# A top-k attention with a feed-forward layer: the first pair of slots projects another unit, two early slots search by pairs, one slot copies x later

## The chip, the cores and the metric

The kernel runs on one core of a Trainium2 chip. The metric is the device time of one execution in microseconds (us). Before the change the median of three runs is 1456.52 us (1456.08 to 1456.63). The engines are named as in the profile: PE is TensorE (PEld its weight loads), DVE is VectorE, ACT is ScalarE, POOL is GpSimd, SP is SyncE, whose queue issues most DMAs.

## What is computed

The reference, cut to what matters:

```python
B, H, S, D = 8, 8, 576, 64
scores = (q @ k.transpose(0, 1, 3, 2)) / np.sqrt(D)
kth = np.partition(scores, -32, axis=-1)[..., -32:-31]
scores = np.where(scores >= kth, scores, -1e9)
attn = np.exp(scores - scores.max(-1, keepdims=True))
attn = attn / (attn.sum(-1, keepdims=True) + 1e-9)
x = (attn @ v).transpose(0, 2, 1, 3).reshape(B * S, H * D)     # 4608 x 512
h = x @ w_in                                                   # 512 x 2048
out = (h / (1 + np.exp(-1.702 * h))) @ w_out                   # 2048 x 512
```

Each row of scores keeps its 32 largest of 576. All matrices are float32.

## The kernel before

**Slots.** The attention is cut into 144 slots, 18 for each batch. A slot holds 128 query rows of two heads (or the 64 left-over rows of two pairs of heads). For slot n the engines do, in this order: TensorE makes the scores (`scores`, L295) into two `s_ps` tiles; ScalarE copies them to `sc` (`copy_scores`, L307); VectorE finds the 32 largest of each row; ScalarE masks (L423) and takes the exponentials with their sums (L431); VectorE inverts the sums (L439, L441); the probabilities are turned, multiplied with v on TensorE (`values`, L526, or `values_at`, L557), and ScalarE copies the result into x (L539, L571).

**Two ways to search.** `topk` works on the 576 scores of a row: eight times MAX8 (L317) and six times MATCH_REPLACE8 (L320) for the two halves of a slot. `topk_of_pairs` works on 288 pairs: `pair_up` puts the greater of each pair into `greater` on VectorE (L336) and starts the lesser on GpSimd (L339), `pair_rest` ends the lesser (L349); then the greater ones are searched as above on half the width (L366, L369), two more rounds go over the lesser ones, and two small reductions (L373, L378) give `top` and the bound `cut`. In the middle of its search it calls `pair_up` for the next slot. After a plain search `bounds` computes `cut` and `low` on GpSimd (L410, L411); after a search by pairs only `low` is left for GpSimd (`lows`, L399).

**Stages.** Slots 0 to 10 are issued one by one by `slot`, with the plain search; their probabilities are turned on TensorE by a scaled identity (`divide`, L448 on GpSimd; `turn`, L468, L471), and ScalarE copies the turned tiles (L476). In these slots the weights are also rounded: `round_piece` gives, for each of 32 pieces, ScalarE operations `size` (L151), `sign` (L153) and `low` (L154), a VectorE `shift` (L152) and two GpSimd operations `finish` (L144, L147). Pieces 0 to 15 are `w_in`; pieces 16 to 31 are the sixteen rows `f` of `w_out`. From slot 11 on `two_slots` issues pairs of slots, with the search by pairs; the probabilities are normalized on GpSimd (`normalize`, L454), split into halves by ScalarE (`split`, L490), and turned by two DMAs in SP's queue (L492, L498).

**Feed-forward.** When four pairs of heads of 128 rows are done, their x is a block (`ready`). A block is worked off in four units of four `f`. `hidden` makes a unit's hidden values `ph` on TensorE (L618); `tanh` on ScalarE takes their tanh (L640), and from slot 11 on also copies `ph` to `h` (L643); `gate` multiplies, on VectorE in slots up to 10 (L655) and on GpSimd afterwards (L652, L653); `project` takes the oldest gated unit from `to_project` and adds four products with `wout` into the block's `po` (L673). After a block's last unit `leave` scales it into `ob` (L681) and sends it out (L683). `may_project` lets a unit be issued only when the `finish` operations of its rows of `wout` are already issued.

**Buffers in PSUM.** `ps_t` has two buffers, shared by the turns, the transposes of q and k for later batches (`prepare_main`, L217, copied by ScalarE at L218; `prepare_ends`, L222), the products `o`, and such `ph` as `hidden` puts there. `ps_h` has one buffer, for `ph`; `ps_p` has one, for `po`. When a block is projected for the first time, `project` gives it `ps_p`, or `ps_h` if another block still has `ps_p`; as long as a block has `ps_h`, `hidden` uses `ps_t`, and for one more call afterwards (`pos["rest"]`).

**Order.** The order is written by hand: in `manual_schedule` each engine runs its instructions in the order in which the program issues them, and waits by semaphores for what they read or overwrite.

In `measure(m)` the bounds of slot m are followed by `pair_rest()` and `gate(aside)`; a pair ends with `tanh(aside)`, `measure(n + 1)`, `project_one()` and `leave_all()`. `opens` is true in the pair of slots 11 and 12, `aside` in all pairs that have slots.

Of the kernel before, what the change touches and what calls it, by code (L numbers as in the profile page):

```python
# [11 lines left out]
F32 = mybir.dt.float32  # L12
# [6 lines left out]
P = 128  # L19
# [11 lines left out]
def kernel(  # L31
# [36 lines left out]
    HALF = S // 2  # L68
# [15 lines left out]
    TURNS = 4  # L84
    SETTLED = 10
    PAIRED = SETTLED + 1
    assert D == 64 and 2 * TAIL == P and C == NP * P and C == PIECE and B % 2 == 0
    assert TOPK == 32 and NP == 4 and NF == 4 and NG == 4 and CC == 4

# [27 lines left out]
    raw = {}  # L117
# [191 lines left out]
    def topk(n):  # L309

        sc = st[n]["sc"]
        top = st[n]["top"] = small.tile([P, 2, TOPK], F32, name="top")
        left = [lefts.tile([P, S], F32, name="left") for _ in range(2)]
        of = lambda r, i: left[i][:] if r else sc[:, i, :]

        def largest(r, i):
            nc.vector.max(top[:, i, 8 * r : 8 * r + 8], of(r, i))  # L317

        def remove(r, i):
            nc.vector.match_replace(left[i][:], top[:, i, 8 * r : 8 * r + 8], of(r, i), LOWEST)  # L320

        ops = []
        for r in range(TOPK // 8):
            ops += [lambda r=r, i=i: largest(r, i) for i in range(2)]
            if r < TOPK // 8 - 1:
                ops += [lambda r=r, i=i: remove(r, i) for i in range(2)]
        return ops
# [3 lines left out]
    def pair_up(n):  # L331

        sc = st[n]["sc"]
        a, b = sc[:, :, 0:HALF], sc[:, :, HALF:S]
        greater[n] = lefts.tile([P, 2, HALF], F32, name="greater", tag="left")
        nc.vector.tensor_tensor(out=greater[n][:], in0=a, in1=b, op=ALU.max)  # L336
        lesser[n] = raws.tile([P, 2, HALF], F32, name="lesser", tag="raw")
        whole = lesser[n][:].bitcast(I32)
        nc.gpsimd.tensor_tensor(out=whole, in0=a.bitcast(I32), in1=greater[n][:].bitcast(I32), op=ALU.subtract)  # L339
        unpaired.append(n)  # L340
# [10 lines left out]
    def topk_of_pairs(n):  # L351

        top = st[n]["top"] = small.tile([P, 2, 2 * TOPK], F32, name="top2", tag="top")
        cut = st[n]["cut"] = small.tile([P, 2], F32, name="cut")
        first, few = greater.pop(n), lesser.pop(n)
        left = lefts.tile([P, 2, HALF], F32, name="left2", tag="left")

        def found(r, i, written=False):
            if r < TOPK // 8:
                at = (8 * r + TOPK) % (TOPK + TOPK // 2)  # L360
                return top[:, i, at : at + 8]
            end = 2 * TOPK - 8 * (r - TOPK // 8) - TOPK
            return top[:, i, end - 1 : end - 9 : -1] if written else top[:, i, end - 8 : end]

        def largest(src, r, i):
            nc.vector.max(found(r, i, True), src[:, i, :])  # L366

        def remove(to, src, r, i):
            nc.vector.match_replace(to[:, i, :], found(r, i), src[:, i, :], LOWEST)  # L369

        def merge():
            both = top[:, :, 0:TOPK].rearrange("p i (s k) -> p i k s", s=2)
            nc.vector.tensor_reduce(  # L373
                out=top[:, :, TOPK + TOPK // 2 :], in_=both, axis=mybir.AxisListType.X, op=ALU.max
            )

        def bound():
            nc.vector.tensor_reduce(  # L378
                out=cut[:], in_=top[:, :, TOPK + TOPK // 2 - 1 :], axis=mybir.AxisListType.X, op=ALU.min, negate=True
            )  # L380

        ops = []
        for r in range(TOPK // 8):
            ops += [lambda r=r, i=i: largest(left if r else first, r, i) for i in range(2)]
            if r < TOPK // 8 - 1:
                ops += [lambda r=r, i=i: remove(left, left if r else first, r, i) for i in range(2)]
        ops += [lambda: pair_up(n + 1) if n + 1 < N else None]
        for r in range(TOPK // 8, TOPK * 3 // 16):
            ops += [lambda r=r, i=i: largest(few, r, i) for i in range(2)]
            if r == TOPK // 8:  # L390
                ops += [lambda r=r, i=i: remove(few, few, r, i) for i in range(2)]
        return ops + [merge, bound]
# [9 lines left out]

    def bounds(n):

        if n >= PAIRED:
            return lows(n)
        top = st[n]["top"]
        cut = st[n]["cut"] = small.tile([P, 2], F32, name="cut")
        low = st[n]["low"] = small.tile([P, 2], F32, name="low")
        nc.gpsimd.tensor_scalar(cut[:], top[:, :, TOPK - 1], -1.0, None, op0=ALU.mult)  # L410
        nc.gpsimd.tensor_tensor(out=low[:], in0=top[:, :, TOPK - 1], in1=top[:, :, 0], op=ALU.subtract)  # L411

    def exponentials(n, between=lambda: None):

        mask(n)
        between()
        exps(n)
# [239 lines left out]
            )  # L657
        to_project.append((th, g, blocks))

    def project(put_off_leaving=False):  # L660

        gT, fs, blocks = to_project.pop(0)
        for x in blocks:
            if not x.done:
                home = "ps_h" if "ps_p" in in_use else "ps_p"
                in_use.append(home)
                x.home = home
                pool_of, tag = (ps_h, "ph") if home == "ps_h" else (ps_p, "po")
                x.po = pool_of.tile([P, C], F32, name="po", tag=tag)
        i = 0  # L670
        for f in fs:
            for x in blocks:
                nc.tensor.matmul(  # L673
                    x.po[:], lhsT=gT[:, i * P : (i + 1) * P], rhs=wout[:, f, :], start=(x.done == 0), stop=(x.done == FC - 1)
                )
                x.done += 1
                i += 1

        def leave(x):
            ob = thp.tile([P, C], F32, name="ob", tag="th")  # L680
            nc.scalar.mul(out=ob[:], in_=x.po[:], mul=0.5 / RAISE**2)  # L681
            for on, to in x.rows:
                nc.sync.dma_start(to, ob[on, :])  # L683

        for x in blocks:
            if x.done == FC:
                in_use.remove(x.home)
                leaving.append(lambda x=x: leave(x))
        if not put_off_leaving:
            leave_all()  # L690
# [49 lines left out]
    def finish_one():  # L740
        unfinished.pop(0)()
# [74 lines left out]
    def slot(n):  # L816
# [7 lines left out]
        if n == 0:  # L824
            for piece in some:
                piece["low"]()
                piece["sign"]()
        else:
            bounds(n - 1)
            exponentials(n - 1, bring_all if n % 4 == 1 else lambda: None)  # L830
            copy_scores(n + 1)
            bring_all()
            while signs:
                signs.pop(0)()
            if 1 < n <= TURNS:
                turn_main(n - 2)
                turn_ends(n - 2)
            for piece in some:
                piece["size"]()
            tanh(False)  # L840
        for i, op in enumerate(topk(n)):
            op()
            if i == 2:
                for _ in range(min(3 if n >= TURNS else 6, len(unfinished))):
                    finish_one()
            if i == 5:
                if n > 0:
                    divide(n - 1)
                while unfinished:
                    finish_one()  # L850
            if i == 10:
                gate(False)
        if n == SETTLED:
            pair_up(n + 1)
            pair_rest()
        for piece in some:
# [2 lines left out]
        if n < NP:  # L859
            for fn, args in preparing:  # L860
                fn(*args)
        if n >= TURNS:
            turn_main(n - 1)
            turn_ends(n - 1)
        if n > 0:
            for piece in some:
                piece["low"]()
        scores(n + 2)
        if n == SETTLED:
            copy_scores(n + 2)  # L870
# [32 lines left out]
    def two_slots(n):  # L903
# [27 lines left out]
        def measure(m):  # L931
            if live(m):
                lows(m)
            pair_rest()
            gate(aside)

        def project_one():
            if may_project(0):
                project(True)

        if opens:
            bounds(n - 1)
            gate(aside)
        if ahead:
            scores(n + 2)
# [26 lines left out]
        for piece in some:  # L972
            piece["shift"]()
            piece["low"]()
            piece["sign"]()
            unfinished.extend(piece["finish"])
        if live(n - 1):
            split(n - 1)
        begin(todo[0])
# [26 lines left out]
        find(n + 1)  # L1006
        if live(n):
            normalize(n)
            split(n)
        begin(todo[1])  # L1010
        if live(n):
            turn_by_dma(n)
        tanh(aside)
        measure(n + 1)
        project_one()
        leave_all()

    with tc.manual_schedule():
# [37 lines left out]
```

## Time and profile before

| | before |
|---|---|
| median of three runs | 1456.52 us |
| the profiled execution | 1456.39 us |
| its span, first to last instruction | 1454.6 us |
| PE busy | 1416.5 us (97%) |
| DVE busy | 1362.5 us (94%) |
| ACT busy | 1158.9 us (80%) |
| POOL busy | 977.6 us (67%) |
| mean granted TensorE clock | 0.986 |

Slot 0's search begins at 9.41 us, slot 10's ends at 132.99 us. In the 40 equal slices of the span (36.4 us each) the page gives, in tenths:

```profile
PE   7789799999999999999999999999999999999998
DVE  7999999999999999999999999999999999999910
PEclk8899899999999999999999999999999999999999
```

A page or a timeline row reads: start, length, engine, line of the kernel, operation, output and inputs with their sizes, count; in brackets the idle time of the engine just before, and whose end released it. The windows give for a stretch of time each engine's busy time, and the clock that TensorE was granted as a share of the full one. The chain is followed back from the last instruction, at each step to what released it or to the instruction before it on its engine.

### The profile page before, as it was taken

The page shows a single profiled execution, that of the slowest core. Times are in us where ns is not written, and L with a number is a line of the kernel's source. Part 1 is how long each engine was busy: PE and PEld are TensorE (multiplying, and loading weights), DVE is VectorE, ACT ScalarE, POOL GpSimd, SP SyncE. Part 2 cuts the span into 40 slices and gives each one's busy share as a digit, 9 for nine tenths or more (in the row PEclk, how much of TensorE's full clock was granted, in tenths as well). Part 3 has the DMA queues.
Part 4 walks back from the last instruction along what each step waited for, and adds up shares of the span by engine and source line. Part 5 has one row for each costly group of instructions (what it writes and reads, how often), then busy time and mean ns, then how long its engine had stood idle before and what let it go on. Part 6 is the DMA issues. An engine that isn't in the chain of part 4 may idle for free.

```text
span 1454.6 us, 29079 instructions
## 1 busy us (share of the span) xinstructions
PE 1416.5 (97%) x9524; PEld 996.4 (68%) x9524; DVE 1362.5 (94%) x4681; ACT 1158.9 (80%) x1862; POOL 977.6 (67%) x1177
## 2 busy tenths in 40 slices
PE   7789799999999999999999999999999999999998
PEld 5667466777666667777666667777666667777665
DVE  7999999999999999999999999999999999999910
ACT  6998787888888887888888888888878888777730
POOL 3788766766677777666777777766777767667610
PEclk8899899999999999999999999999999999999999
DMA  7442467777777867777677767767677776645430
GB/s 224 136 161 75 127 154 191 189 189 180 176 198 184 188 170 191 186 198 177 170 194 182 183 170 195 202 174 189 166 203 189 180 182 179 161 133 130 138 89 15
DMA packets 521272, 244.40 MB, mean 168 GB/s; under 512 B 457376, under 2 KB 495264, under 8 KB 521120
## 3 DMA queue, kind: packets, MB, share of 16 engines
q1 hardware_dynamic: 520688, 242.25, 64.4%
q8 instruction: 75, 1.23, 0.3%
q14 instruction: 77, 0.63, 0.2%
q10 hardware_dynamic: 432, 0.30, 0.1%
HBM read 45.09 MB, written 103.42 MB: 102 GB/s over the span
## 4 chain that ended last, share of the span: by engine, by line
PE 87%; DVE 10%; ACT 2%; POOL 0%; issue 0%; DMA 0%; DVEq 0%; POOLq 0%; ACTq 0%
PE ph L618 33%; PE po L673 32%; PE o L557 10%; PE s_ps L295 10%; DVE top L317 4%; DVE left L320 3%; DVE top L366 1%; DVE left L369 1%; ACT sc L490 0%; ACT sc L423 0%; ACT pr L431 0%; DVE wout L152 0%; PE none L169 0%; ACT sc L307 0%; DMA pt<-rows 0%
## 5 line engine op out<-in xcount | busy, mean ns | idle before, releaser
L618 PEld LDWEIGHTS ph<-xT,win 128*128 128x128 f32 x3520 | 484.2, 191 | 85.2 <-issue 54.6
L618 PE MATMUL ph<-xT,win 128*128 128x128 f32 (+1 forms) x3520 | 537.1, 309 | 0.5 <-ACT xT L574 0.5
L673 PE MATMUL po<-wout,th 128*128 128x512 f32 x1152 | 521.0, 595 | 5.6 <-POOL wout L147 5.6
L490 ACT COPY sc<-pr 128x2304 uint16<-128x2304 uint16 x134 | 283.1, 2113 | 170.3 <-POOL pr L454 170.3
L673 PEld LDWEIGHTS po<-wout,th 128*128 128x128 f32 x1152 | 213.6, 191 | 219.0 <-issue 205.8
L366 DVE MAX8 top<-left 128x8 f32<-128x288 f32 x798 | 323.2, 446 | 0.0
L339 POOL TENSOR_TENSOR lesser<-sc,greater 128x576 int32<-128x576 int32 x133 | 188.4, 1417 | 179.8 <-DVE greater L336 179.8
L454 POOL TENSOR_SCALAR pr<-pr,rden 128x576 f32<-128x576 f32 x268 | 196.6, 746 | 126.7 <-DVE top L373 77.7
L369 DVE MATCH_REPLACE8 left<-top,left 128x288 f32<-128x288 f32 x532 | 231.3, 442 | 0.0
L431 ACT ACTIVATE pr<-sc,low 128x576 f32<-128x576 f32 x288 | 220.8, 774 | 0.0
L366 DVE MAX8 top<-lesser 128x8 f32<-128x288 f32 x532 | 214.9, 445 | 0.0
L423 ACT ACTIVATE sc<-sc,cut 128x576 f32<-128x576 f32 x288 | 207.4, 774 | 6.2 <-POOL cut L410 6.2
L307 ACT ACTIVATE sc<-s_ps 128x576 f32<-128x576 f32 x288 | 170.9, 648 | 34.2 <-PE s_ps L295 32.6
L349 POOL TENSOR_TENSOR lesser<-lesser,sc 128x576 int32<-128x576 int32 x133 | 187.8, 1412 | 0.1
L295 PE MATMUL s_ps<-qk_t 64*128 64x288 f32 (+1 forms) x1280 | 183.7, 433 | 0.5 <-ACT qk_t L218 0.3
L653 POOL TENSOR_TENSOR th<-th,h 128x512 f32<-128x512 f32 x131 | 167.5, 1279 | 10.9
L295 PEld LDWEIGHTS s_ps<-qk_t 64*128 64x128 f32 (+1 forms) x1280 | 100.2, 179 | 79.2 <-issue 59.0
L557 PE MATMUL o<-pt,v_l 128*64 128x128 f32 (+1 forms) x2400 | 145.8, 265 | 2.1 <-DMA pt<-rows 1.9
L557 PEld LDWEIGHTS o<-pt,v_l 128*64 128x64 f32 x2400 | 121.4, 137 | 29.5 <-issue 17.7
L336 DVE TENSOR_TENSOR greater<-sc 128x576 f32<-128x576 f32 x133 | 131.9, 992 | 0.0
L652 POOL TENSOR_SCALAR th<-th 128x512 f32<-128x512 f32 x131 | 81.5, 622 | 59.7 <-ACT th L640 59.7
L640 ACT ACTIVATE th<-ph 128x512 f32<-128x512 f32 x144 | 85.5, 593 | 38.0 <-PE ph L618 33.9
(78 smaller groups left out, 1365.5 us busy)
## 6 DMA issues: line engine op xcount, KB each, us to landing
rows<-sc SPq DMA_DIRECT2D x134, 576.0 KB, 3.2
qk_rows<-halves SPq DMA_DIRECT2D x48, 256.0 KB, 2.8
qk_l<-in_q_dram SPq DMA_DIRECT2D x64, 128.0 KB, 3.4
raw<-in_moe_w_in_dram SPq DMA_DIRECT2D x16, 512.0 KB, 4.7
v_l<-in_v_dram SPq DMA_DIRECT2D x32, 256.0 KB, 3.7
raw<-in_moe_w_out_dram SPq DMA_DIRECT2D x16, 512.0 KB, 3.5
out_dram<-ob SPq DMA_DIRECT2D x32, 256.0 KB, 2.9
qk_l<-in_k_dram SPq DMA_DIRECT2D x62, 128.0 KB, 3.4
```

The costliest lines, as they stand in the source:

```text
L295: nc.tensor.matmul(ps[i][rows, c, 0:HALF], lhsT=qT[b, hps[p]][on, cols], rhs=kT[b, hps[p]][on, FIRST[i] + c * HALF : FIRST[i] + (c + 1) * ...
L339: nc.gpsimd.tensor_tensor(out=whole, in0=a.bitcast(I32), in1=greater[n][:].bitcast(I32), op=ALU.subtract)
L349: nc.gpsimd.tensor_tensor(out=whole, in0=whole, in1=b.bitcast(I32), op=ALU.add)
L366: nc.vector.max(found(r, i, True), src[:, i, :])
L369: nc.vector.match_replace(to[:, i, :], found(r, i), src[:, i, :], LOWEST)
L423: nc.scalar.activation(sc[:, i, :], sc[:, i, :], AF.Prelu, bias=cut[:, i : i + 1], alpha=HUGE)
L431: nc.scalar.activation(pr[:, i * S : (i + 1) * S], sc[:, i, :], AF.Exp, bias=low[:, i : i + 1], accum_out=den[:, i : i + 1],)
L454: nc.gpsimd.tensor_scalar(pr[:, i, :], pr[:, i, :], st[n]["rden"][:, i : i + 1], 1.0, op0=ALU.mult, op1=ALU.mult)
L490: nc.scalar.copy(out=halves, in_=pr[:].bitcast(U16).rearrange("p (k h) -> p h k", h=2))
L557: nc.tensor.matmul(o[j * D : (j + 1) * D, cols], lhsT=main[:, j, c, :] if c < NF else tail[:, j, :], rhs=pt[:, MAIN[j] + c if c < NF else ...
L618: nc.tensor.matmul(ph[:, i * many * P : (i + 1) * many * P], lhsT=win[:, c, f * P : (f + 1) * P], rhs=xs[:, first : first + step * (many - ...
L673: nc.tensor.matmul(x.po[:], lhsT=gT[:, i * P : (i + 1) * P], rhs=wout[:, f, :], start=(x.done == 0), stop=(x.done == FC - 1))
```

## The change

- `by_pairs` says which slots are searched by pairs: now also slots 1 and 2 (`EARLY`). Their `lesser` lives in the pool of `sc` rather than that of the raw weights. The slot before such a slot calls `bounds` for itself, then `pair_up` and `pair_rest`, at the end of its own search; that holds for slot 10 too, whose `bounds` came after slot 11's `pair_up` before.
- Slot 5 (`TURNS + 1`) copies x (`bring_all`) behind the exponentials and not between the mask and them, and gates its unit after operation 13 of its search, not 10. Slot 4 issues two of its three `low` operations ahead of the turns of slot 3.
- In the first pair, slot 11's `measure` finishes the pieces that are left (one whole piece of `wout`) and gates nothing; the last piece's `finish` follows at once instead of during the search of slot 12. `measure` of slot 14 gates twice.
- At the end of the first pair `project(True, 1)` takes the second unit in `to_project`, the first of the next block, where `project_one` took the oldest, the last of the first block. That one is projected by the next pair.
- In the pair of slots 13 and 14 the `tanh` of the second half stands ahead of slot 13's `split`.

The core of the diff:

```diff
+    EARLY = (1, 2)
+    by_pairs = lambda n: n in EARLY or PAIRED <= n < N
...
-        lesser[n] = raws.tile([P, 2, HALF], F32, name="lesser", tag="raw")
+        home, tag = (scp, "sc") if n in EARLY else (raws, "raw")
+        lesser[n] = home.tile([P, 2, HALF], F32, name="lesser", tag=tag)
...
-        ops += [lambda: pair_up(n + 1) if n + 1 < N else None]
+        ops += [lambda: pair_up(n + 1) if PAIRED < n + 1 < N else None]
...
-    def project(put_off_leaving=False):
+    def project(put_off_leaving=False, which=0):
-        gT, fs, blocks = to_project.pop(0)
+        gT, fs, blocks = to_project.pop(which)
...
-            bounds(n - 1)
-            exponentials(n - 1, bring_all if n % 4 == 1 else lambda: None)
+            if not by_pairs(n):
+                bounds(n - 1)
+            exponentials(n - 1, bring_all if n % 4 == 1 and n > TURNS + 1 else lambda: None)
+            if n == TURNS + 1:
+                bring_all()
...
-        for i, op in enumerate(topk(n)):
+        for i, op in enumerate(topk_of_pairs(n) if n in EARLY else topk(n)):
...
-            if i == 5:
+            if i == (10 if n in EARLY else 5):
...
-            if i == 10:
+            if i == (13 if n == TURNS + 1 else 10):
                 gate(False)
-        if n == SETTLED:
+        if by_pairs(n + 1):
+            bounds(n)
             pair_up(n + 1)
             pair_rest()
...
+        lows_of = [piece["low"] for piece in some] if n > 0 else []
+        if n == TURNS:
+            for _ in range(2):
+                lows_of.pop(0)()
...
+            if opens and m == n:
+                finish_one()
+                finish_one()
+                pair_rest()
+                return
             pair_rest()
             gate(aside)
+            if m == SETTLED + 4:
+                gate(aside)
...
-            bounds(n - 1)
             gate(aside)
...
+        while unfinished:
+            finish_one()
...
+        if n == SETTLED + 3:
+            tanh(aside)
+        if live(n):
             split(n)
...
-        project_one()
+        if opens:
+            project(True, 1)
+        else:
+            project_one()
```

More of the change, by code (lines that the diff above doesn't have):

```diff
@@ L403, in bounds @@
     def bounds(n):
-        if n >= PAIRED:
+        if by_pairs(n):
             return lows(n)
@@ L864, in slot @@
             turn_ends(n - 1)
-        if n > 0:
-            for piece in some:
-                piece["low"]()
+        for low in lows_of:
+            low()
         scores(n + 2)
```

## The prediction

> **What bounds the kernel now.** I read the page first, then the chain that ended last in order of time, then the timelines of the engines up to 230 us, then the windows for the granted clock. By the page, TensorE carries 87% of the chain, VectorE 10%.
>
> ```profile
> PE 87%; DVE 10%; ACT 2%; POOL 0%; issue 0%; DMA 0%; DVEq 0%; POOLq 0%; ACTq 0%
> ```
>
> From the windows (columns: length, busy time and count of PE, PEld, DVE, ACT, POOL, granted clock, DMA):
>
> ```profile
> 79.89:81.48 1.59, 0.00 (x0) 0.00 (x0) 1.55 (x6) 1.59 (x6) 0.84 (x3) 1.00 0.82 260
> 81.48:84.90 3.42, 2.67 (x22) 2.31 (x24) 3.42 (x9) 3.33 (x8) 3.34 (x4) 1.00 0.32 101
> 90.91:93.00 2.09, 0.00 (x1) 0.01 (x1) 2.06 (x6) 2.09 (x7) 1.64 (x3) 1.00 0.46 123
> 94.40:97.80 3.40, 3.40 (x19) 2.46 (x17) 3.40 (x8) 2.77 (x7) 2.69 (x3) 0.53 0.57 179
> 230.00:1442.00 1212.00, 1211.51 (x8033) 844.48 (x8032) 1145.15 (x4073) 964.74 (x1489) 817.99 (x994) 1.00 0.68 173
> ```
>
> The last row is the most important: from 230 us on TensorE is never idle, so what is lost or won before that moves the end by as much, and nothing later takes it up. The four rows above it show the clock: TensorE idle for 1.59 us kept the full clock, idle for 2.09 us it ran the stretch from 94.4 to 97.8 at half.
>
> Before 230 us the chain is this:
>
> ```profile
> 156.03 1.41 POOL lesser L339
> 157.44 1.45 POOL pr L454 x2
> 158.89 0.02 issue
> 158.91 2.11 ACT sc L490
> ...
> 179.50 0.66 PE tp L217 x4
> 180.15 3.57 PE ph L618 x32
> ```
>
> So from slot 0 to 180 us not TensorE sets the pace but VectorE, then GpSimd and ScalarE. TensorE's own stop, for the rounded `wout`, lies inside that stretch:
>
> ```profile
> 146.47 1.98 PE L673 MATMUL po<-wout,th 128*128 128x512 f32 x4
> 153.52 2.07 PE L673 MATMUL po<-wout,th 128*128 128x512 f32 x2 [5.07 <-POOL wout L147]
> ```
>
> **The change, part by part.** Units are numbered in the order they are hidden: 0-3 are the first block's, 4-7 the next one's. All times are those of the trace before.
>
> *Slots 1 and 2 by pairs.* A plain search takes 9.65 us of VectorE (19.72 to 29.64 less 0.27 for L439, L441). By pairs it is 8.23 (134.65 to 140.10, 141.00 to 142.58, 143.74 to 144.94) plus `pair_up`, whose 0.74 takes 0.66 of the queue; beside GpSimd work it took up to 1.60. So each slot gains between 0.76 and -0.2. I take 1.3 for both. GpSimd gets L339 and L349 in each (1.41 + 1.42); its idle 3.85 and 3.84 us before L410 at 29.81 and 40.39 hide them. Without that cover the scaled identities (L448) would be late for TensorE at 39.71, 1 us later by my count. `lesser` in the four `sc` buffers waits for nothing: the one it takes was last read a slot earlier.
>
> *Slot 5.* VectorE waits twice there:
>
> ```profile
> 68.37 0.17 DVE L439 TENSOR_SCALAR some<-den 128x2 f32<-128x2 f32 x1 [1.06 <-ACT pr L431]
> 72.77 0.69 DVE L655 SCALAR_TENSOR_TENSOR th<-th,ph 128x512 f32<-128x512 f32 x1 [0.54 <-ACT th L640]
> ```
>
> Two L154 (1.14) ahead of slot 4's last turns fill ScalarE's waits of 0.59 and 1.12 at 60 us. Slot 4's mask, 1.3 ahead from slots 1 and 2 and some 0.7 from these waits, starts near 62.95 instead of 65.01, its exponentials end at 65.85 (0.37 of x between them is gone too), and the gate comes three operations later: both waits go. But x now follows, 0.37 behind 65.85, so unit 0 starts on TensorE at about 66.25 instead of 66.41, and the turn behind it lets ScalarE finish its copies (L476) at about 72.7 instead of 73.94. ScalarE has no idle time from 62.7 to 100 us except behind such turns. Slot 5's exponentials therefore end only some 1.3 earlier, and VectorE, ahead by 1.3 + 1.06 + 0.54, waits for them in slot 6. The lead that reaches slot 11 lies between 0 and 3.1 (2 x 0.76 + 1.60); I take 1.4, ScalarE's.
>
> *Slot 10.* `bounds` goes ahead of `pair_up`: L423 can start at 135.9, not 137.71. Worth nothing: ScalarE then waits until 141.65 for scores from TensorE, which is busy without a break.
>
> *First pair (slots 11, 12).* TensorE projects unit 4, whose pieces of `wout` and gate are long done, so the stop of 5.07 + 0.53 goes. It isn't won: the next scores need L307 at 152.52, the transposes behind them L218, and the values of slot 11 need its rows turned by DMA, which took 7.43 us from the end of L490 (160.93 to 168.36). What moves that is GpSimd's queue: the gate of unit 6 (0.62 + 1.28) leaves, the last piece ends at 153.7, L339 starts there and not at 156.03, L490 ends at 158.65, the values start at 166.1 instead of 168.36. L349 of slot 12 comes later, 151.05; its reader is due at 152.25. The gates of units 6 and 7 land in idle time (3.90 before 172.19), long before their projects at 183.67 and 195.70. `ob` (L681, 0.50, with its output DMA on SP, 0.54) moves behind the exponentials of slot 13, where ScalarE idles for 3.38. VectorE's 1.43 at 164.40 goes too, since exponentials of slot 12 end near 161.5. With `tanh` ahead of L490 in slot 13 the 1.01 before L217 at 179.50 goes. TensorE would be ready for unit 9 at 176.5 rather than 179.99.
>
> *Where the stop goes.* Unit 4 opens its block while the first one is unfinished, so the block gets `ps_h` and keeps it up to unit 7. `hidden` then puts units 9 and 11 into `ps_t`, whose two buffers hold the q and k transposes (L217). Their first matmul must now wait for L218 of q, which stands in ScalarE's queue behind a pair's mask and exponentials; before, only L222 waited for that, after the unit.
>
> Unit 9: the reciprocal of slot 13 at 173.25 (174.69 less 1.43), L454 as before 0.17 behind it, 1.47 long: 174.9; L490 2.02, L423 1.34, L431 1.52, L218 0.50: 180.25. So unit 9 starts at 180.3, 0.3 later than before, after 3.8 us of an idle TensorE. What the first pair won is gone.
>
> Unit 11: the rows before are
>
> ```profile
> 199.33 0.60 ACT L681 ACTIVATE ob<-po 128x512 f32<-128x512 f32 x1 [1.19 <-PE po L673]
> 199.83 1.43 ACT L423 ACTIVATE sc<-sc,cut 128x576 f32<-128x576 f32 x2
> ...
> 202.68 1.05 ACT L218 COPY qk_t<-tp 128x512 f32<-128x512 f32 x2
> ```
>
> L681 waits for the project that ends at 199.13, so the chain follows TensorE itself and no lead shortens it: the first copy is there at 203.2, unit 11 started at 200.01. Cost 3.25.
>
> *Clock.* Stops of 3.8 and 3.25 exceed the 2.09 that dropped it. After that drop, and after 3.58 us idle before 45.95, one stretch of 3.4 us ran at half: 1.65 us each (scores at 46.3 2.27 for 1.24, values 1.69 for 1.09). Bounds: 0, and two such stretches, 3.4 (57 to 63 us). I take 1.65 each, 3.3. "TensorE: Matmul & The Clock Gate" of the skill (What's actually happening) has the clock halved after an idle window of some 3.4 us. That speaks against the change. Read strictly, unit 11's stop would escape, and the sum would be 1.65 less; the row of 2.09 us disagrees with so long a threshold.
>
> **Sum.** -1.4 (lead) + 0.3 (unit 9) + 3.25 (unit 11) + 3.3 (clock) = +5.45. The profiled execution took 1456.39 (span 1454.6 and 1.79 around it), 0.13 below the median of 1456.52. So 1461.8.
>
> **Rivals.** *The clock stays up* (not slower). Place: both stops. If their idle time falls so between the clock's stretches that none has more than the 1.59 that was harmless, 3.3 vanishes: +2.15, 1458.5. For it: that row. Against: 3.8 and 3.25 are twice as long, and behind every stop over 2 us before 160 us the trace has a stretch at half clock.
>
> *The buffers come free in time* (faster). If the copy of q were done when TensorE arrives, unit 9 would start 3.5 earlier, unit 11 without a stop: -1.4 - 3.5, 1451.5. It needs ScalarE 3.8 and 3.25 us ahead. For it: ScalarE idles 3.38 before 176.36. Against: that idle time waits for GpSimd and VectorE, and L681 ties the second to TensorE.
>
> *No lead, or a longer cold stretch.* If the early pairing brings nothing (ScalarE is busy nearly throughout), +6.85, 1463.2; with a second half-clock stretch at one stop besides, 1464.9. That is the change failing at one of the things it does.
>
> **Numbers.** Within 0.2% means 2.9 us, about what a measurement tells from none. Forecast 0.50 (own range 1459 to 1464: lead 0.5 to 3, a clock stretch more or less partly hit), clock up 0.21, buffers free 0.09, no lead or long cold 0.20. Slower: 0.46 + 0.02 + 0.20 = 0.68; same: 0.04 + 0.18 = 0.22; faster: 0.01 + 0.09 = 0.10. The range takes in the first and third rival and half the way to the second: 1455 to 1465.5.
>
> **What would show it.** The 5.07 before L673 gone; unit 9's and unit 11's L618 each behind an idle time of 3 to 4 us put down to ScalarE's copy into `qk_t`, with a clock near 0.5 behind them; slot 10's search ending 1 to 2 us earlier; a wait of some 1.5 at L439 in slot 6. If those L618 start without a wait, or the clock stays at 1.00 behind them, I am wrong.

## The result and the profile after

| | before | after |
|---|---|---|
| median of six runs each | 1456.48 us (1456.05 to 1456.93) | 1462.47 us (1458.69 to 1465.88) |
| the profiled execution, its span | 1456.39, 1454.6 us | 1462.82, 1461.0 us |
| granted clock of that execution | 0.986 | 0.987 |

The ratio is 1.0036 with a 95% interval of 1.0026 to 1.0047: the change makes the kernel slower, by 6.0 us between the medians (5.2 by the ratio). The median is 0.7 above the forecast of 1461.8 and inside its own range. In later experiments the kernel before had medians of 1456.40 to 1456.59 beside the new kernels. The six runs of the changed kernel spread over 7.2 us, the six of before over 0.9, and the 19 to 25 of before in the later groups over 3.4 to 3.7.

Lines of the changed kernel are two or three higher than before: `hidden` L621 (was L618), `project` L676 (L673), the leaving `ob` L684 (L681), mask L426 (L423), exponentials L434 (L431), `split` L493 (L490), the copy of q L220 (L218), `tanh` L643 (L640).

On the page the chain that ended last now has 1% of DMA in it, where before it rounded to 0% (one transfer, 4.53 us at 220.33):

```profile
PE 86%; DVE 10%; ACT 2%; DMA 1%; issue 1%; POOL 0%; SPq 0%; DVEq 0%; POOLq 0%; ACTq 0%
```

TensorE before 215 us, from its timeline in the changed kernel (in brackets its idle time just before and what ended it):

```profile
144.73 3.70 PE L676 MATMUL po<-wout,th 128*128 128x512 f32 x8
151.49 2.41 PE L297 MATMUL s_ps<-qk_t 64*128 64x288 f32 x8 [3.06 <-ACT sc L309]
...
165.85 1.98 PE L560 MATMUL o<-pt,v_l 128*64 128x128 f32 x16 [2.02 <-DMA pt<-rows]
...
170.01 3.84 PE L621 MATMUL ph<-xT,win 128*128 128x128 f32 x32
...
180.34 3.84 PE L621 MATMUL ph<-xT,win 128*128 128x128 f32 x32 [2.18 <-ACT qk_t L220]
...
203.75 5.42 PE L621 MATMUL ph<-xT,win 128*128 128x128 f32 x32 [3.12 <-ACT qk_t L220]
209.01 0.27 PE L224 MATMUL tp<-ident,qk_l 128*128 128x128 f32 x1
```

The stop of 5.07 us for the rounded `wout` is gone: unit 4's project runs through. Units 8, 9 and 11 are the last three L621. Units 9 and 11 now wait for ScalarE's copy of q, as forecast. Unit 11 also takes 5.42 us for its 32 products where unit 9 takes 3.84. The windows say why (length, busy time and count of PE, PEld, DVE, ACT, POOL, then the granted clock):

```profile
163.00:169.70 6.70, 4.67 (x36) 3.59 (x32) 6.70 (x24) 4.53 (x7) 4.64 (x5) 0.51 0.41 131
178.16:180.34 2.18, 0.00 (x1) 0.00 (x0) 1.19 (x6) 2.18 (x7) 0.65 (x1) 1.00 1.04 287
180.34:184.00 3.66, 3.65 (x32) 3.66 (x33) 3.59 (x14) 0.44 (x1) 3.30 (x5) 1.00 0.54 121
200.63:203.75 3.12, 0.00 (x0) 0.00 (x1) 2.09 (x10) 3.12 (x8) 1.41 (x1) 0.99 0.69 156
203.75:207.15 3.40, 3.40 (x16) 3.40 (x17) 3.33 (x14) 0.43 (x1) 3.30 (x5) 0.51 1.10 237
...
230.00:1448.00 1218.00, 1216.05 (x8076) 848.47 (x8077) 1150.84 (x4093) 970.98 (x1499) 819.63 (x995) 1.00 0.68 173
```

Behind unit 9's stop (2.18 us) the clock stayed at 1.00. Behind unit 11's (3.12 us) it was 0.51 for 3.4 us. The values and scores of 163 to 169.7 also ran at half. From 230 us on TensorE idles for 1.95 us of 1218 where before it had 0.49 of 1212; some 0.5 of that belongs to a wait for turned rows that both kernels have (ahead of 230.47 here, of 224.90 before).

Unit 11's wait, in ScalarE's timeline, is the chain that the prediction wrote down from the rows of before:

```profile
199.79 0.60 ACT L684 ACTIVATE ob<-po 128x512 f32<-128x512 f32 x1 [1.31 <-PE po L676]
200.29 1.43 ACT L426 ACTIVATE sc<-sc,cut 128x576 f32<-128x576 f32 x2
...
203.13 1.05 ACT L220 COPY qk_t<-tp 128x512 f32<-128x512 f32 x2
```

Unit 9's wait hangs on something else than forecast. The chain that ended last, in order of time (pieces of it from 153 to 181 us):

```profile
159.80 6.01 DMA pt<-rows
...
165.85 2.40 PE o L560 x20
168.26 1.83 PE s_ps L297 x8
170.08 3.78 PE ph L621 x32
...
173.89 0.60 ACT th L643
174.49 0.48 ACT h L646
174.96 2.01 ACT sc L493
...
179.82 0.48 ACT qk_t L220
...
180.34 1.72 PE ph L621 x13
```

The turned rows of slot 11 landed after 6.01 us. Then values and scores ran at half clock, unit 8 followed, and `tanh` of unit 8, which the change puts ahead of slot 13's `split`, held the split until unit 8 was done.

The account against before, by the starts of the same instructions: unit 9 +0.35 us (180.34 for 179.99); unit 11 +3.74 (203.75 for 200.01), so 3.39 more; the L224 behind it +5.43 (209.01 for 203.58), so 1.69 more, the half clock (5.42 for 3.74). That holds to 233 us. One more wait follows, which before doesn't have:

```profile
250.71 1.09 PE L560 MATMUL o<-pt,v_l 128*64 128x128 f32 x16 [1.02 <-DMA pt<-rows]
```

The four parts make 6.45; the spans differ by 6.4. At the start of the kernel the change did better than forecast. In VectorE's timeline both waits of slot 5 are gone (72.98 for 75.43 at the shift behind the gate), and slot 11's pairing, at 132.99 before, stands at

```profile
130.71 0.74 DVE L338 TENSOR_TENSOR greater<-sc 128x576 f32<-128x576 f32 x1
```

a lead of 2.28 us.

### The profile page after: what moved, and what is told of

It reads as the page before. It is cut to its first block, busy times and chain, and to the rows that moved or that the text cites. A ratio compares the mean times of both kernels' runs of the same rounds, so it can differ in the third digit from the quotient of the medians.

```text
span 1461.0 us, 29107 instructions
## 1 busy us (share of the span) xinstructions
PE 1416.9 (97%) x9524; PEld 998.5 (68%) x9524; DVE 1361.6 (93%) x4703; ACT 1159.8 (79%) x1862; POOL 985.0 (67%) x1181
## 4 chain that ended last, share of the span: by engine, by line
PE 86%; DVE 10%; ACT 2%; DMA 1%; issue 1%; POOL 0%; SPq 0%; DVEq 0%; POOLq 0%; ACTq 0%
PE ph L621 33%; PE po L676 32%; PE o L560 10%; PE s_ps L297 10%; DVE top L319 3%; DVE left L322 2%; DVE top L369 2%; DVE left L372 1%; DMA pt<-rows 1%; ACT sc L493 0%; DVE lesser L372 0%; DVE win L154 0%; ACT sc L426 0%; DVE greater L338 0%; ACT pr L434 0%
## 5 line engine op out<-in xcount | busy, mean ns | idle before, releaser
L621 PEld LDWEIGHTS ph<-xT,win 128*128 128x128 f32 x3520 | 485.9, 192 | 91.7 <-issue 54.8
L621 PE MATMUL ph<-xT,win 128*128 128x128 f32 (+1 forms) x3520 | 539.2, 310 | 6.3 <-ACT qk_t L220 5.3
L676 PE MATMUL po<-wout,th 128*128 128x512 f32 x1152 | 518.5, 593 | 0.0
L493 ACT COPY sc<-pr 128x2304 uint16<-128x2304 uint16 x134 | 283.1, 2113 | 160.2 <-POOL pr L457 160.2
L676 PEld LDWEIGHTS po<-wout,th 128*128 128x128 f32 x1152 | 213.4, 190 | 211.9 <-issue 206.5
L369 DVE MAX8 top<-left 128x8 f32<-128x288 f32 x810 | 328.1, 446 | 0.0
L372 DVE MATCH_REPLACE8 left<-top,left 128x288 f32<-128x288 f32 x540 | 234.8, 442 | 0.0
L434 ACT ACTIVATE pr<-sc,low 128x576 f32<-128x576 f32 x288 | 220.8, 773 | 0.0
L369 DVE MAX8 top<-lesser 128x8 f32<-128x288 f32 x540 | 218.1, 444 | 0.0
L426 ACT ACTIVATE sc<-sc,cut 128x576 f32<-128x576 f32 x288 | 207.3, 773 | 2.0 <-POOL cut L413 2.0
L643 ACT ACTIVATE th<-ph 128x512 f32<-128x512 f32 x144 | 85.4, 593 | 40.9 <-PE ph L621 36.2
```

The lines of the kernel that those rows point to most:

```text
L426: nc.scalar.activation(sc[:, i, :], sc[:, i, :], AF.Prelu, bias=cut[:, i : i + 1], alpha=HUGE)
L434: nc.scalar.activation(pr[:, i * S : (i + 1) * S], sc[:, i, :], AF.Exp, bias=low[:, i : i + 1], accum_out=den[:, i : i + 1],)
L493: nc.scalar.copy(out=halves, in_=pr[:].bitcast(U16).rearrange("p (k h) -> p h k", h=2))
L621: nc.tensor.matmul(ph[:, i * many * P : (i + 1) * many * P], lhsT=win[:, c, f * P : (f + 1) * P], rhs=xs[:, first : first + step * (many - ...
L676: nc.tensor.matmul(x.po[:], lhsT=gT[:, i * P : (i + 1) * P], rhs=wout[:, f, :], start=(x.done == 0), stop=(x.done == FC - 1))
```

## The experiments

The theory: the order of the projects costs the time, since it sends units 9 and 11 to `ps_t` behind the copy of q, while the other edits gain. Each experiment is the changed kernel with a small edit unless it says otherwise. "before" below is the kernel before on the same chip, 19 to 25 runs in each group.

**e1_order_back: the order alone undone.**

```diff
-        if opens:
-            project(True, 1)
-        else:
-            project_one()
+        project_one()
```

> The changed kernel with one thing undone: at the end of the first pair the oldest unit (3) is projected again, so the next block gets ps_p and units 9 and 11 go where they went before. Theory (the loss sits in the two waits of units 9 and 11 for the copy of q, and in the clock behind them): both waits are gone, TensorE stops again for wout in the first pair, some 5 us, but that stop costs nothing because the values of slot 11 wait for GpSimd, ScalarE and the DMA anyway; 1452 to 1455 us. Rival (the moved finish operations and gates of the first pair, or the early slots, cost the time): the waits go, the time stays at 1459 or above. Second rival (the stop for wout was worth its 5 us): 1460 or more, with the stop on the chain.

Measured: 1452.76 us (1451.85 to 1452.93), ratio 0.9973 (0.9963 to 0.9983): faster than before, and 9.7 us faster than the changed kernel. TensorE's timeline:

```profile
147.88 1.13 PE L676 MATMUL po<-wout,th 128*128 128x512 f32 x2 [0.54 <-POOL wout L149]
152.25 2.07 PE L676 MATMUL po<-wout,th 128*128 128x512 f32 x2 [3.24 <-POOL wout L149]
...
175.34 3.74 PE L621 MATMUL ph<-xT,win 128*128 128x128 f32 x32
...
195.63 3.74 PE L621 MATMUL ph<-xT,win 128*128 128x128 f32 x32
```

The stop for `wout` is back (3.78 us), and yet unit 9 starts 5.0 us earlier than in the changed kernel and unit 11 8.1 us earlier, both without a wait and at full clock. The stop that the new order saves lies in a stretch where TensorE waits anyway; what it pays lies where TensorE sets the end.

**e5_order_alone: the order alone done**, on the kernel before.

```diff
-        project_one()
+        if opens:
+            project(True, 1)
+        else:
+            project_one()
```

> The kernel before with one edit: the first pair projects unit 4 (to_project.pop(1)) instead of unit 3; no early pairing, no reordering of slot 5, gates and measure as before. Theory (the order of the projects is what costs, through the buffers): the stop of 5 us for the rounded wout at 150 us goes, but units 9 and 11 go to ps_t and wait for the copy of q. Without the lead unit 9 starts later than in the changed kernel (180.34): some 2 to 3 us behind the 179.99 of before, unit 11 waits 3.1 to 3.3 us, and one to two half-clock stretches of 1.6 us follow: 1464 to 1466 us, span 1462 to 1464. Rival (the order wins its stop, and what costs lies in the other edits): not above 1454.

Measured: 1463.96 us (1463.13 to 1466.33), ratio 1.0054 (1.0039 to 1.0069), at the lower edge of what the theory had. In its profile (the run of 1466.33):

```profile
183.08 5.47 PE L618 MATMUL ph<-xT,win 128*128 128x128 f32 x32 [2.66 <-ACT qk_t L218]
...
208.12 5.46 PE L618 MATMUL ph<-xT,win 128*128 128x128 f32 x32 [3.12 <-ACT qk_t L218]
```

Unit 9 is 3.09 us later than before, unit 11 waits the same 3.12, and here both run at half clock. With e1 this settles the main question from both sides: the order costs 7.6 us on the old kernel and 9.7 on the rest of the change.

**e4_start_only: the start alone**; slots 1, 2, 4, 5 and 10 as changed, the pairs from slot 11 on as before.

```diff
-            if opens and m == n:
-                finish_one()
-                finish_one()
-                pair_rest()
-                return
-            if m == SETTLED + 4:
-                gate(aside)
-        while unfinished:
-            finish_one()
-        if n == SETTLED + 3:
-            tanh(aside)
-        if opens:
-            project(True, 1)
-        else:
-            project_one()
+        project_one()
```

> The change's start alone (slots 1 and 2 by pairs, slots 4 and 5, bounds ahead of pair_up in slot 10), with the first pairs as in the kernel before. Theory: slot 11's pair_up comes 2.3 us earlier, as in the changed kernel's trace, and the lead goes through to the end, because VectorE, GpSimd and ScalarE set the pace up to 180 us: 1453.5 to 1455 us. Rival (the lead is lost in the first pair, where TensorE and the DMAs wait anyway): 1456 to 1457 us. If the start cost time: above 1457.

Measured: 1455.25 us (1454.85 to 1455.96), ratio 0.9994 (0.9986 to 1.0003): a gain of 1.3 us that its interval doesn't tell from none, between the theory and its rival. The profile has a lead of 1.84 us at slot 11 (131.15) and still 1.93 at unit 9 (178.06), and then a wait of 0.66 us at 243 us. So the start brings about one us to the end, and the other edits of the pairs bring the rest of e1's gain, 2.5 us.

**e8_no_early: e1 with slots 1 and 2 searched plainly.**

```diff
-    EARLY = (1, 2)
+    EARLY = ()
```

> The fastest kernel so far (the changed kernel with the first block's last unit projected in the first pair again, 1452.76) but with EARLY = (), so that slots 1 and 2 search plain scores; slots 4 and 5 keep the changed order. It splits the lead of 2.28 us that the changed kernel has at slot 11: theory (slots 1 and 2 bring the larger part, 1.05 at slot 3): 0.6 to 1.2 us slower, 1453.3 to 1454.0, slot 11's pairing starting some 0.6 to 1.2 later. Rival (slots 4 and 5 bring all of it, since only 0.6 was left behind slot 4): within 0.3 us of 1452.76.

Measured: 1453.12 us (1452.03 to 1454.49), ratio 0.9978 (0.9969 to 0.9987): 0.36 above e1, between the two expectations, and the intervals overlap. The profiles say more than the times. VectorE pairs slot 11 at 132.29, and in e1 at 131.15. So the early pairing brings 1.14 us of the lead, and slots 4, 5 and 10 bring 0.70. But e1 has a wait of 0.71 us for turned rows at 240.68, and e8 has none of 0.25 or more between 223 and 300 us: e1 is 1.71 us ahead at the unit before that wait (223.27 for 224.98) and 1.09 at the unit behind it (243.09 for 244.18). So 0.6 us is given back there. The spans still differ by 1.5; e8's profiled execution is its longest run, and why the medians differ by only 0.36 isn't shown.

**e7_unit11_only: `ps_h` for unit 11 alone**, and **e2_unit11_home**, the same with an edit that reached further.

```diff
+        if n == SETTLED + 7:
+            pos["rest"] = 1
```

> The changed kernel, but unit 11 alone gets ps_h back (one line ahead of its hidden call in the pair that starts with slot 17); unit 9 and every later block keep their buffers. Theory: unit 11 waits for nothing but the drained output of an older block, its 3.1 us stop and the half-clock stretch of 1.6 us behind it go, unit 9 stays as it is: 1457.5 to 1459.5 us. Rival (the loss of the earlier trial of this, 1461.5, was not from the buffers of later blocks): 1461 to 1463.

Measured: 1459.01 us (1456.47 to 1460.87), ratio 1.0017 (1.0008 to 1.0027), as the theory had it. Unit 11 starts without a wait at 200.11 and takes 3.82. e2 put the rule into `hidden`:

```diff
-        if many > 1 or pos["other"] or "ps_h" in in_use:
+        if many > 1 or pos["other"]:
             pos["rest"] = 2
+        elif "ps_h" in in_use:
+            pos["rest"] = 1
```

> The changed kernel, but hidden goes back to ps_h one call sooner, so unit 11 takes ps_h and unit 9 still ps_t. Theory: the 3.12 us before unit 11 go (it waits for ob alone, which is ready when the transposes are done), with them the 1.6 us of half clock behind; unit 9 as it was: 1457 to 1459 us, no run above 1462. Rival (unit 11's wait only takes the place of another one behind it): that other wait shows up, 1462 as it is.

Measured: 1461.49 us (1457.9 to 1463.72), ratio 1.0035 (1.0023 to 1.0047): a miss. (Its lines from `hidden` on are two higher again.) Unit 11's wait went there too (203.02, 3.82), but later blocks lost `ps_t` as well, with new waits of 0.7 us each, 2.1 in all, for `ob`; and in the profiled execution the half clock fell on unit 9 instead:

```profile
181.27 5.47 PE L623 MATMUL ph<-xT,win 128*128 128x128 f32 x32 [2.19 <-ACT qk_t L220]
```

A stop of 2.19 us with a drop, beside 2.18 us without one in the changed kernel. e2 by itself would have spoken against the theory; e7 shows that it was the reach of the edit.

**e12_ob_behind: `ob` out of the way.** Buffers and TensorE's order stay; only the copy L684 and its transfer go behind the copy of q.

```diff
         hidden(ps_t if opens else None)
+        if n == SETTLED + 7:
+            leave_all()
...
-        leave_all()
+        if n != SETTLED + 5:
+            leave_all()
```

> The changed kernel, but the copy of the finished block out of PSUM (L684) and its output transfer are put behind the copy of q in the pair that starts with slot 17; buffers and order of TensorE as in the change. Theory (unit 11's chain follows TensorE only because L684 stands ahead of the mask, as the prediction has it): the mask starts at about 198.5 and not 200.3, the copy of q is there 1.8 us earlier, the stop goes from 3.1 to about 1.3 and the clock stays up behind it: 1459.0 to 1461.0. Rival (the mask waits for something else, VectorE's search or GpSimd's bound): stop stays at 3, 1462 to 1463.

Measured: 1459.97 us (1458.71 to 1462.44), ratio 1.0028 (1.0018 to 1.0038), as the theory had it. ScalarE:

```profile
197.99 1.45 ACT L426 ACTIVATE sc<-sc,cut 128x576 f32<-128x576 f32 x2
...
200.85 1.05 ACT L220 COPY qk_t<-tp 128x512 f32<-128x512 f32 x2
201.79 0.61 ACT L684 ACTIVATE ob<-po 128x512 f32<-128x512 f32 x1
```

and TensorE:

```profile
201.47 3.84 PE L621 MATMUL ph<-xT,win 128*128 128x128 f32 x32 [1.22 <-ACT qk_t L220]
```

The stop falls from 3.12 to 1.22, and the clock stays up behind it. This is the link of the chain that tied unit 11 to TensorE's own end of the project before it.

**e6_project_first: other work in the stops.** The two pairs issue the project ahead of the hidden unit.

```diff
+        first = n in (SETTLED + 5, SETTLED + 7)
+        if first:
+            project_one()
         hidden(ps_t if opens else None)
-        if len(to_gate) == units:
+        if len(to_gate) == units and not first:
             project_one()
...
-        if len(to_gate) > units:
+        if len(to_gate) > units and not first:
             project_one()
```

> The changed kernel, but in the two pairs that hide units 9 and 11 the project (3.4 us of TensorE, on work that is ready) is issued ahead of the hidden unit instead of behind it, so that TensorE has this to do while ScalarE makes the copy of q. Theory (the stops are waits for that copy and the clock drops because TensorE idles in them): L621 of units 9 and 11 starts with at most 0.5 us of idle time ahead of it, 2.2 and 3.1 us come back, and the half-clock stretch of 1.6 behind unit 11 too: 1455 to 1457.5 us. Rival (what the stops cost is lost elsewhere anyway, in the tail of VectorE and GpSimd that sets the end of the pairs): 1461 to 1463, as the changed kernel.

Measured: 1458.55 us (1455.28 to 1459.94), ratio 1.0013 (1.0003 to 1.0022). That is 3.9 below the changed kernel, and 1 us above the range. Both stops are gone; unit 9:

```profile
175.40 3.60 PE L676 MATMUL po<-wout,th 128*128 128x512 f32 x8
178.84 3.73 PE L621 MATMUL ph<-xT,win 128*128 128x128 f32 x32
```

The profile is one of its shorter runs (1456.11). In it the scores behind unit 11 stand 9.0 us earlier than in the changed kernel (203.66 for 212.65), and 2.3 of that is lost again by the end (span 1454.3 for 1461.0). Some 1.8 of the 2.3 is clock, by an estimate from its mean, 0.91 from 210 to 230 us where the changed kernel has 1.00; its waits of 0.4 us and more behind 204 us, 2.97 in all, are as long as there (2.93).

**e3_warm: the clock alone.** Twelve filler products on data that is there, ahead of each of the two units.

```diff
+        if n == SETTLED + 5 or n == SETTLED + 7:
+            stay_warm(12)
```

> The changed kernel with twelve matmuls of the identity into ps_p ahead of unit 9 and of unit 11, some 3 us each: the waits for the copy of q stay, but TensorE is not idle in them. Theory (the spread of its runs, 1458.7 to 1465.9, and 1.6 us of its median are the clock behind the stops): granted clock 1.00 behind both units, 1458.5 to 1461 us, runs within 2 us of each other. Rival (the clock plays no part in the loss): median at 1462 or above, spread as before.

Measured: 1462.51 us (1460.9 to 1463.01), ratio 1.004 (1.0028 to 1.0052). The gain that was expected didn't come. Unit 8, unit 9, the filler ahead of unit 11 (its twelve products are 24 instructions) and unit 11:

```profile
170.72 3.84 PE L621 MATMUL ph<-xT,win 128*128 128x128 f32 x32
...
181.39 3.74 PE L621 MATMUL ph<-xT,win 128*128 128x128 f32 x32
...
201.41 2.84 PE L171 MATMUL none<-ident 128*128 128x128 f32 x24
204.69 3.84 PE L621 MATMUL ph<-xT,win 128*128 128x128 f32 x32 [0.44 <-ACT qk_t L220]
```

Both units run at full clock (1.00) in this execution. But they start 1.05 and 0.94 us later than in the changed kernel's first profile, which takes most of the 1.6 us that was saved once. In the main that isn't the filler: unit 8 is already 0.71 us late here (170.72 for 170.01), ahead of any filler, so at most 0.34 at unit 9 is the filler's; and unit 11 still waits 0.44 us for the copy of q behind it. Why the median gained nothing stays open with one profile. What did change is the spread: 2.1 us in five runs instead of 7.2 in six.

**after_again: the changed kernel once more.**

> The changed kernel once more, unedited, for how far its executions differ among themselves. Theory (what varies is how many of the stops let the clock fall, some 1.6 us each, and how long the turned rows of slot 11 take to land): median 1461.5 to 1463.0, spread again over 4 us, and the profile may show another set of half-clock stretches than the first one. Rival (the width of the first runs was an accident): spread below 2 us.

Measured: 1462.23 us (1461.18 to 1467.11), ratio 1.0047 (1.0034 to 1.0059), with a spread of 5.9, as the theory had it. The profile of the same instructions is another one:

```profile
164.87 1.09 PE L560 MATMUL o<-pt,v_l 128*64 128x128 f32 x16 [0.73 <-DMA pt<-rows]
...
179.22 5.21 PE L621 MATMUL ph<-xT,win 128*128 128x128 f32 x32 [3.79 <-ACT qk_t L220]
...
204.00 3.84 PE L621 MATMUL ph<-xT,win 128*128 128x128 f32 x32 [3.12 <-ACT qk_t L220]
```

The rows of slot 11 took 1.7 us less to land (4.28 from 160.59 to 164.87). Unit 9 starts 1.12 us earlier behind a longer stop of 3.79, with the half clock there; unit 11's stop of 3.12, the same as before, now keeps the clock. Against before: unit 9 -0.77, unit 11 +3.99, and a wait of 1.12 at 249.49; the span is 1460.1.

**e10_tanh_behind: unit 8's `tanh` behind the split again.**

```diff
-        if n == SETTLED + 3:
-            tanh(aside)
```

> The changed kernel without its two lines 'if n == SETTLED + 3: tanh(aside)', so that unit 8's tanh and copy stand behind the split of slot 13 (L493) on ScalarE again, not ahead of it. Theory (unit 9's stop of 2.18 us comes from L493 waiting behind a tanh that waits for TensorE's unit 8, 174.85 where GpSimd's rows were ready near 171.5): L493 of slot 13 starts 2 to 3 us earlier, the copy of q 1.5 to 2 us earlier, unit 9's stop is at most 0.5, unit 11's stays 3.1: 1460.0 to 1461.0. Rival (the stop comes from the late values of slot 11 and the lead alone): unit 9's stop stays about 2, 1462 to 1463.

Measured: 1462.76 us (1460.55 to 1464.06), ratio 1.0039 (1.0026 to 1.0052): a miss; time and stop are those of the rival. ScalarE:

```profile
172.51 2.11 ACT L493 COPY sc<-pr 128x2304 uint16<-128x2304 uint16 x1 [2.65 <-POOL pr L457]
174.53 0.59 ACT L643 ACTIVATE th<-ph 128x512 f32<-128x512 f32 x1
...
175.48 1.45 ACT L426 ACTIVATE sc<-sc,cut 128x576 f32<-128x576 f32 x2
...
178.34 1.05 ACT L220 COPY qk_t<-tp 128x512 f32<-128x512 f32 x2
```

L493 starts 2.3 us earlier, as expected, but `tanh` and the copy now stand between split and mask, so the copy of q gains 1.4 on the first profile (179.72) and only 0.3 on the second (178.60). And TensorE was ready earlier too (rows landed by 164.11): its stop is 2.66, and both units ran at half clock. The moved `tanh` held up the split in the profiles in which the rows of slot 11 landed late (after, e3), and not in the repeat and e12, where GpSimd's rows came last.

**e11_both: e7 and e10 together.**

> Both edits at once: unit 8's tanh behind the split of slot 13, and ps_h for unit 11 alone. Theory (the two stops, 2.2 and 3.1, and the half-clock stretches behind them are what the order of the projects costs, and the stop for wout is won): neither unit waits more than 0.5 us, 1453 to 1456. Rival (only the order back gives more): not below 1457.

Measured: 1457.34 us (1456.4 to 1460.36), ratio 1.0009 (1.0000 to 1.0017), 1.3 us above the range, where the rival had it. Unit 9 waits 0.77, unit 11 not at all, the clock stays up behind both:

```profile
165.87 1.98 PE L560 MATMUL o<-pt,v_l 128*64 128x128 f32 x16 [2.18 <-DMA pt<-rows]
...
179.12 3.84 PE L621 MATMUL ph<-xT,win 128*128 128x128 f32 x32 [0.77 <-ACT qk_t L220]
...
199.24 3.82 PE L621 MATMUL ph<-xT,win 128*128 128x128 f32 x32
```

The rows landed late here, so TensorE came late to unit 9, and the stop is short for that reason. In e1 unit 9 starts at 175.34: it doesn't need the copy of q. That is what e11 can't win back as long as unit 9 is in `ps_t`: 3.8 us. The fastest version is e1, which beats both kernels: all of the change but the order of the projects (e8, 0.36 us behind it, isn't told apart).

## Why the prediction held

- **The stop for `wout` goes and isn't won.** Held. Unit 4's project has no stop, and unit 9 starts where it did, within a us (180.34 and 179.22 for 179.99). e1 shows the price: with the stop in place unit 9 can start at 175.34.
- **Units 9 and 11 wait in `ps_t` for the copy of q.** Held in every kernel with the new order, except where an edit was made against it (e7, e2, e12, e6).
- **Unit 11, 3.25.** Held: the stop is 3.12 in the changed kernel, in its repeat, in e5 and in e10, whatever the lead was (-0.33 in e5 to 2.32 in e10), and 3.39 by the starts. That it follows TensorE through L684 is shown by e12.
- **Lead, 1.4.** Mis-sized: 2.28 and 1.81 in the two profiles of the changed kernel. The early slots were right (1.3 forecast, 1.14 by e1 and e8). What failed is the statement that slot 5's exponentials end only some 1.3 earlier because unit 0 starts on TensorE at 66.25 and holds up ScalarE's turns. Part of unit 0 ran at 64.65, the rest from 65.84, and ScalarE's copies L479 ended at 71.69, 2.25 before those of before (73.94, forecast 72.7). So the wait of 1.5 forecast for slot 6 didn't come.
- **Unit 9, +0.3 beside that lead, so 178.9 in the sum.** Measured 180.34 and 179.22 in the changed kernel, 178.34 to 178.97 in e7, e10 and e12. The forecast took 7.43 us from split to values from before; the first profile has 9.04 (154.79 + 2.02 to 165.85), the repeat 7.28. In the first profile the path was another one, too: the forecast's copy of q hangs on VectorE's reciprocal, GpSimd and the split, and in the repeat the split does wait for GpSimd (1.49 us); in the first profile the copy hangs on the turned rows, on the values and scores at half clock (4.16 us from the values to unit 8, 2.41 in the repeat) and on unit 8's `tanh`. The rank of the `tanh` was read as a gain of 1.01 at L217; here it held up the split, which e10 shows 2.3 us earlier without it. The stop itself, 3.8 in the forecast, was 2.18 and 3.79.
- **Clock, 3.3, one half-speed stretch at each stop.** Mis-sized: each of the two profiles has one, worth 1.6 and 1.4, and at the other stop the clock stays up, which the prediction named as a sign of being wrong. e5 and e10 have both. The rows it rested on (2.09 us idle, then half clock; 1.59 us harmless) are no rule: 3.12 us kept the clock in the repeat, and 1.44 didn't in e6 (last section).
- **Not foreseen: the wait of 1.0 at 250 us.** It is in every kernel with the early pairing (0.66 to 1.12), and in none of the three without it (before, e5, e8). Which link of that slot is late was not traced. It speaks against the prediction's reading that nothing behind 230 us takes up what is won before: in e4, 1.93 us ahead at unit 9, 1.1 is left at the end.

So the place and the two waits were right, and the sum of 5.45 stood against 6.4 and 5.5 in the two profiles because of errors that cancel: in the first profile the 1.45 that unit 9 is later than in the sum, and 1.0 from a wait not foreseen, against 1.6 of clock too much. That the sum came so near is in part luck. Of the rivals, a clock that stays up at both stops (1458.5) is near the two shortest runs, 1458.69 and 1458.77, which have the highest mean clock (0.990); no trace of them was taken. Buffers that come free in time are refuted by both profiles, and "no lead" by 130.71.

## What to carry to other kernels

Removing the largest stop of an engine can be worth nothing where other waits of the same stretch end later; see first whether the next thing that must start there becomes ready earlier. A change of order also changes which buffers are open at the same time: follow every later allocation, since two units that had waited for nothing here came to wait for another engine's copy, with stops that begin 33 and 56 us after the edited project. And a change of several parts is worth splitting: here the parts without the order gain 3.8 us, and the order loses 9.7.

## What the runs showed of the hardware

**The same stop drops the clock in one execution and not in the next.** Stops ahead of unit 9 and unit 11, with the length of the unit behind (about 3.8 at full clock):

| stop, us | no drop | drop |
|---|---|---|
| 0.44 to 1.22 | e3 (unit 11, behind filler), e11 (unit 9), e12 (unit 11) | |
| 2.18 to 2.19 | after (3.84) | e2 (5.47) |
| 2.66 to 2.71 | | e5, e7, e10, e12 (all unit 9, 5.46 to 5.47) |
| 3.12 | repeat (3.84) | after (5.42), e5 (5.46), e10 (5.26) |
| 3.79 | | repeat (5.21) |

A drop lasts about 3.4 us (clock 0.51 and 0.52 over that time in after and e2) and costs 1.4 to 1.6, by the lengths of the units. Elsewhere a still shorter stop had one. In e6 the clock was 1.00 from 218.96 to 220.50 and 0.50 from there to 223.90, behind

```profile
218.96 0.33 PE L224 MATMUL tp<-ident,qk_l 128*128 128x128 f32 x1 [1.44 <-ACT qk_t L220]
219.43 1.77 PE L297 MATMUL s_ps<-qk_t 64*128 64x288 f32 x8 [0.15 <-ACT qk_t L220]
```

So a drop can also begin when TensorE has been at work again for 1 us or more; before the change, the stop of 2.09 us ended at 93.00 and the stretch at half began near 94.4. The Trainium skill ("TensorE: Matmul & The Clock Gate", What's actually happening) has a window of some 3.4 us that runs freely and isn't started by the program. The length of the slow stretches and the chance in the table agree with that. Its condition of an idle window at the least, read as one with no work at all, doesn't: stops of 2.19 and 2.7 us dropped the clock, and in e6 one of 1.44.

**The same transfer lands after 4.3 or 6.0 us.** Up to 170 us the instructions of after, its repeat, e6 and e11 are the same. From the issue of slot 11's turning transfer to the values that wait for it they took 6.05 (159.80 to 165.85), 4.28 (160.59 to 164.87), 4.48 (159.70 to 164.18) and 5.96 (159.91 to 165.87). e2, e3, e7, e10 and e12 are edited only behind that, too: 6.05 and 5.95 in e2 and e3, 4.36 in e10, and at most 4.54 and 4.48 in e7 and e12, whose values didn't wait. So of nine executions four are near 6.0, five at most 4.54, and none between. Why was not found.

**The spread.** Up to two clock drops of 1.6 at the stops make 3.2 us of the 7.2 by which the changed kernel's runs differ, and the five runs of e3, whose profile has neither, spread over 2.1. But e6 and e11, whose profiles have no drop at these units either, spread over 4.7 and 4.0, so the stops alone don't make the spread. That the rest comes from the landing and from half-clock stretches elsewhere is possible, but only argued: the mean clock of the changed kernel's first six runs falls from 0.990 to 0.983 as they lengthen, and one stretch of 3.4 us at half lowers the mean of 1461 us by 0.0012.
